# Attention with two mixtures of experts: weights decoded by shifts and ors alone, half chunks scored on a block diagonal

## The chip, the cores and the metric

The kernel runs on one core of one Trainium2 chip. The metric is the device time of one execution in microseconds (us). In the profile PE is TensorE's matrix multiply, PEld its weight load, DVE VectorE, ACT ScalarE, POOL GpSimd and SP SyncE, whose queue issues most DMAs.

## What is computed

```python
# q, k, v: (4 batches, 8 heads, 576, 64) float32; tau a scalar
scores = (q @ k.T) / sqrt(64)
scores = where(scores >= rowmax - tau, scores, -1e9)
attn = exp(scores - rowmax);  attn /= attn.sum + 1e-9
x = (attn @ v) as (2304 tokens, 512)
h = max(x @ w_in, 0);  x = (h * h) @ w_out       # w_in 512 x 2048, w_out 2048 x 512, both float64
e = argmax(x @ w_gate)                           # 8 experts
out[token] = softmax_e * sigmoid(x @ w_output_gate)_e * (max(x @ w1[e], 0) @ w2[e])
```

The weights w_in and w_out arrive as float64. The kernel reads each as two 32-bit words and makes a float32 of them, which it then splits.

## The kernel before

All matrix products that need float32 accuracy run on TensorE in a reduced format, with each operand split into a high part and the remainder (two arrays), so that one product takes three or four passes.

**Order of the work.** The program writes no loops of its own: it adds tasks to a graph (`g.add`), each with an engine, an estimated duration, what it reads and writes and a key. A planner then puts them in order, engine by engine: of the tasks that could start soonest it takes the one with the lowest key. Keys count planned time, T0 = 3 us for one chunk. A task may have a release (`rel`) before which it is not planned. Buffers come from pools; a task whose pool has no free slot is not a candidate. What the planner fixes is only the order in each engine's queue; on the chip each queue runs in that order and waits on semaphores.

**Attention.** There are 16 pairs of heads (4 batches, 4 pairs each), and 9 chunks of 128 query rows for each pair: four of head 0, one half chunk that holds the last 64 rows of both heads (step 4, `hd == 2`), four of head 1. For each chunk: scores (PE, line 630), row maximum (DVE, 639), exponential (ACT, 642), threshold and mask with row sum (647, 651), division (POOL 656 and 662, DVE 659), five transposes (PE, 712), their evacuation in two parts (ACT 729, DVE 732), and after the last chunk of a group the product with v (PE, 755 or 773).

For each pair `t_load` fetches k, q and v; `t_qk` transposes k and q (PE, 568), writes the high part (ACT 576, 578) and the remainder (DVE 584, 586) into one buffer `xy` of four planes; `t_op` copies them by DMA (lines 600 and 603, on SP's queue) into the operands of the scores: for each head an array with high part above and remainder below, so that the 128 rows of the contraction hold both and two passes give all four products. `opA` (head 0) has two slots, `opB` (head 1) one. The half chunk takes two passes from each of the two arrays over both halves of 288 keys: eight matmuls.

**First mixture.** After the four pairs of a batch, `t_h` multiplies with w_in (PE, line 853, 32 units of 12 matmuls a batch), applies max(., 0) (ACT, 859) and stores to scratch r_scr (DMA, 862, three buffers). These units are mixed into the next batch's attention; those of the last batch follow the attention. Then `t_g` and `t_y` (953, 968) read it back and multiply with w_out, gating follows, and the experts (lines 1194 to 1292).

**Decoding.** `t_w` decodes one of 32 weights blocks (16 of w_in, 16 of w_out; 128 x 512 words each): fetch (DMA 818), ACT scales the high word by 2^-112, which rebases the exponent (825), and turns the low word into a number (827); DVE takes the sign (828), shifts the rebased word left by 3 and puts the sign in (830), and isolates the power of two (832); POOL multiplies that with the low word's number (834); POOL (w_in) or DVE (w_out) adds it (836); ACT makes the high part (837) and POOL or DVE the remainder (839). The 16 of w_in are released at 40 + 5i us of planned time and lie among the attention of batches 0 and 1; those of w_out follow the attention.

Of the kernel before, what the change touches and what calls it, by code (L numbers as in the profile page):

```python
# [257 lines left out]
def moa(ctx, tc, q, k, v, tau, w_in, w_out, wg, wog, w1, w2, ctab, coln, out):  # L258
    nc = tc.nc
# [27 lines left out]
    SQ = 640  # L287
# [3 lines left out]
    W1, W2 = 40, 5.0  # L291
# [50 lines left out]
    MEMF, MEMR = 10544, 25856  # L342
# [104 lines left out]
    ATT = at = at + 512  # L447
# [10 lines left out]
    assert at <= DEC, at  # L458
    at = mk("raw", DEC, 4, [P, 2, 512], F32, 2)
# [33 lines left out]
    for i in (1, 2):  # L493
        nc.gpsimd.memset(ALL["opB"].slots[0].view[:, i, 0:64].bitcast(F32), 0.0)
# [13 lines left out]
    raws, vh, xys, opb, xTb, xfb, wb = {}, {}, {}, {}, {}, {}, {}  # L508
# [40 lines left out]
    def t_qk(pr, nm, part, key):  # L549

        raw = raws[pr, nm]
        xy = xys.setdefault(pr, None) or new("xy", pr)
        xys[pr] = xy

        if nm == "k":
            xi, yi = 0, 3
            cs, n0 = ((0, 1, 2), 0) if part == 0 else ((3, 4), 384)
        else:
            xi, yi = 1, 2
            cs, n0 = ((4, 0, 1), 0) if part == 0 else ((2, 3), 320)  # L560
# [12 lines left out]
        def hi():  # L573
            X = xy.t[:, xi, n0 : n0 + n]
            if nm == "k":
                nc.scalar.activation(X, ps.t[:, :n], AF.Copy)
            else:
                nc.scalar.activation(X, ps.t[:, :n], AF.Copy, scale=qsc)

        def lo():  # L580
            X = xy.t[:, xi, n0 : n0 + n].bitcast(F32)
            Y = xy.t[:, yi, n0 : n0 + n]
# [6 lines left out]
        g.add("ACT", c_act(n, True, nm == "q"), hi, [ps], [(xy, xi, part)], key - 1)  # L589
        g.add("DVE", c_dve(n), lo, [ps, (xy, xi, part)], [(xy, yi, part)], key - 1)  # L590

    def t_op(pr, j, key):

        xy = xys[pr]
        buf = opb[pr, j] = new("opB" if j else "opA", f"{pr}")
        rows = slice(64 * j, 64 * j + 64)
        z = 64 if j else 0

        def top():
            nc.sync.dma_start(buf.t[0:64, :, z : z + S].bitcast(F32), xy.t[rows, 0:3].bitcast(F32))  # L600

        def bot(i, src):
            nc.sync.dma_start(buf.t[64:128, i, z : z + S].bitcast(F32), xy.t[rows, src].bitcast(F32))

        parts = lambda *xs: [(xy, x, p) for x in xs for p in range(2)]
        dma(top, 64 * 3 * S * 4, parts(0, 1, 2), [(buf, 0)], key)
        for i, src in ((0, 3), (1, 2), (2, 1)):
            dma(lambda i=i, src=src: bot(i, src), 64 * S * 4, parts(src), [(buf, 1, i)], key)

    def t_chunk(n, key):  # L610
# [5 lines left out]
        if hd == 2:  # L616
            cols = [(1, 0, P), (0, 0, 64)]
        else:
            cols = [(hd, 64 + 64 * hd + QOFF[c], P)]
        seq = [(j, i, q0, m) for j, q0, m in cols for i in (1, 2)]  # L620
        if hd == 2:
            seq = [seq[0], seq[2], seq[3], seq[1]]
        heads = (0, 1) if hd == 2 else (hd,)

        def mm():
            for i, (j, slot, q0, m) in enumerate(seq):
                o = opb[pr, j].t
                z = 64 if j else 0
                for hf in range(2):
                    nc.tensor.matmul(  # L630
                        s.t[:m, hf, :HALF],
                        o[:, slot, q0 : q0 + m],
                        o[:, 0, z + hf * HALF : z + (hf + 1) * HALF],
                        start=(i == 0),
                        stop=(i == len(seq) - 1),
                    )
# [27 lines left out]
        ob = [(opb[pr, j], x) for j in heads for x in (0,)] + [(opb[pr, j], 1, i) for j in heads for i in range(3)]  # L664
        if n < EARLY:
            xy = xys[pr]
            q0 = 64 + QOFF[c]

            def mm():
                i = 0  # L670
                for qx, kx in ((1, 0), (1, 3), (2, 0), (2, 3)):
                    for hf in range(2):
                        nc.tensor.matmul(
                            s.t[:, hf, :HALF], xy.t[0:64, qx, q0 : q0 + P], xy.t[0:64, kx, hf * HALF : (hf + 1) * HALF],
# [4 lines left out]
            rd = [(xy, x, p) for x in (0, 3) for p in range(2)] + [(xy, x, 0 if c < 2 else 1) for x in (1, 2)]  # L679
            g.add("PE", c_pe(HALF) * 8, mm, rd, [s], key)  # L680
        else:
            g.add("PE", c_pe(HALF) * 2 * len(seq), mm, ob, [s], key + K("scores", pr))
# [119 lines left out]
    def t_w(i, key):  # L802

        fc = i % NFC
        raw, av, sg, sc, lf = new("wraw", i), new("wa", i), new("wb", i), new("wc", i), new("wd", i)
# [16 lines left out]
        ts = nc.vector.tensor_scalar  # L822

        dma(fetch, 524288, [], [raw], key - 6, rel=W1 + W2 * i if i < NFC else NCH * T0 - 20)
# [8 lines left out]
        early = i < NFC  # L833
        g.add("POOL", 1.3, lambda: nc.gpsimd.tensor_tensor(sc.t, sc.t, lf.t, op=ALU.mult), [lf], [sc], key)
        rest = ("POOL", 1.3, nc.gpsimd) if early else ("DVE", c_dve(512), nc.vector)
        g.add(*rest[:2], lambda: rest[2].tensor_tensor(av.t, av.t, sc.t, op=ALU.add), [sc], [av], key)
        g.add("ACT", c_act(512), lambda: nc.scalar.activation(w.t[:, 0], av.t, AF.Copy), [av], [(w, 0)], key)
        g.add(*rest[:2],
# [459 lines left out]
    def pair_prep(pr, key):  # L1298
# [116 lines left out]
```

## Time and profile before

| | us |
|---|---|
| median of 3 runs | 1059.66 (1058.43 to 1063.24) |
| profiled execution | 1060.76 |
| its span, first to last instruction | 1059.0 |
| PE busy | 995.3 (94%) |
| DVE busy | 719.3 (68%) |
| ACT busy | 664.8 (63%) |
| POOL busy | 426.3 (40%) |

The span is cut into stages by the clock of the trace: attention runs from about 10 to 500 us, w_in is decoded between 53 and 250 us, w_out between 449 and 570 us, the last batch's first product ends at 562 us, the second product runs to about 750 us, and the experts from there to the end. A stage's busy times say which engine has no slack there; the share over the whole span does not. The busy time of PE counts pipelined matmuls that overlap, so matmuls for each us are read beside it.

### The profile page before, as it was taken

The numbers are of one execution on the slowest core, as the hardware profiler recorded it, in microseconds if no ns is written. First come the engines' busy times: TensorE is split into PE (matmuls) and PEld (weight loads), VectorE is DVE, ScalarE is ACT, GpSimd is POOL, SyncE is SP. The second block draws the span as 40 slices with busy tenths as digits, with TensorE's granted clock in tenths as the row PEclk, the third lists the DMA queues.
The fourth block names the chain that finished last, engine by engine and source line by source line (L and its number), as shares of the span: only waits on it lengthen the run. The fifth ranks groups of instructions, "written<-read, shape, count | busy, mean of one in ns | idle before, by whom it ended". The sixth has DMA issues, their size and how long they took to land.

```text
span 1059.0 us, 19173 instructions
## 1 busy us (share of the span) xinstructions
PE 995.3 (94%) x6300; PEld 883.7 (83%) x6300; DVE 719.3 (68%) x1607; ACT 664.8 (63%) x1379; POOL 426.3 (40%) x757
## 2 busy tenths in 40 slices
PE   6888888889999999999999999999999999999995
PEld 5566678879999999989888888888789998888884
DVE  4789899887777788785964334444677758767720
ACT  5778877766666667675854455444664668767730
POOL 1368898897566665563331000000112211211200
PEclk9989999999999999999999999999999999999998
DMA  6656656544556445553783333443667868877700
GB/s 146 150 151 158 157 130 175 147 117 109 143 142 147 126 125 130 136 157 111 223 237 117 100 100 100 114 117 103 195 190 244 284 211 287 274 253 270 267 20 24
DMA packets 158848, 169.05 MB, mean 160 GB/s; under 512 B 55823, under 2 KB 121615, under 8 KB 158738
## 3 DMA queue, kind: packets, MB, share of 16 engines
q1 hardware_dynamic: 154498, 157.20, 52.5%
q0 software_dynamic: 4096, 10.52, 3.1%
q8 instruction: 52, 0.85, 0.4%
q14 instruction: 58, 0.48, 0.1%
q10 hardware_dynamic: 144, 0.00, 0.0%
HBM read 110.86 MB, written 29.56 MB: 133 GB/s over the span
## 4 chain that ended last, share of the span: by engine, by line
PE 66%; DVE 8%; DMA 7%; issue 7%; POOL 6%; ACT 4%; SPq 0%; POOLq 0%; DVEq 0%; ACTq 0%
PE bank L968 17%; PE bank L853 12%; PE bank L1282 8%; PE bank L1232 7%; PE bank L630 5%; PE bank L712 5%; PE bank L755 5%; DMA memf<-in_moe_w_dram 2%; POOL memf L662 2%; PE bank L1252 1%; DMA out_dram<-memf 1%; PE bank L568 1%; PE bank L773 1%; DVE memf L639 1%; DMA memf<-in_moe_w_in_dram 1%
## 5 line engine op out<-in xcount | busy, mean ns | idle before, releaser
L853 PE MATMUL bank<-memr,w 128*128 128x288 f32 x1536 | 231.9, 300 | 5.3 <-ACT memf L859 4.7
L853 PEld LDWEIGHTS bank<-memr,w 128*128 128x128 f32 x1536 | 210.6, 189 | 9.9 <-ACT memf L859 7.5
L968 PE MATMUL bank<-w,memr 128*128 128x512 f32 x648 | 157.4, 394 | 0.0
L968 PEld LDWEIGHTS bank<-w,memr 128*128 128x128 f32 x648 | 119.1, 188 | 23.5
L651 DVE SCALAR_TENSOR_TENSOR memf<-bank,memf 128x576 f32<-128x576 f32 x144 | 116.4, 810 | 19.0 <-ACT memf L642 18.6
L712 PE MATMUL bank<-ident,memf 128*128 128x128 f32 x720 | 107.7, 280 | 20.0 <-DVE memr L732 8.4
L630 PE MATMUL bank<-memr 128*128 128x288 f32 (+1 forms) x632 | 116.2, 313 | 10.6 <-DVE memf L651 8.7
L639 DVE TENSOR_REDUCE memf<-bank 128x1 f32<-128x576 f32 x144 | 106.9, 748 | 7.8 <-PE bank L630 4.6
L712 PEld LDWEIGHTS bank<-ident,memf 128*128 128x128 f32 x720 | 83.8, 143 | 31.4 <-DVE memr L732 6.2
L662 POOL TENSOR_SCALAR memf<-memf 128x576 f32<-128x576 f32 x128 | 97.6, 764 | 28.0 <-DVE memf L659 21.0
L630 PEld LDWEIGHTS bank<-memr 128*128 128x128 f32 (+1 forms) x632 | 91.7, 188 | 17.1 <-DVE memf L651 14.9
L729 ACT ACTIVATE memr<-bank 128x640 fp32r<-128x640 f32 (+1 forms) x140 | 89.5, 648 | 25.4 <-PE bank L712 23.0
L642 ACT ACTIVATE memf<-bank,memf 128x576 f32<-128x576 f32 x144 | 105.3, 733 | 0.2
L732 DVE TENSOR_TENSOR memr<-bank,memr 128x512 fp32r<-128x512 f32 (+1 forms) x140 | 87.3, 631 | 21.9 <-ACT memr L729 21.3
L1073 POOL DMA_INDIRECT lst<-memf x18 | 17.9, 996 | 203.5 <-DVE memf L1059 140.2
L1232 PE MATMUL bank<-memr,w 128*128 128x256 f32 x564 | 89.0, 283 | 1.5 <-DVE memr L1242 1.4
L953 DVE TENSOR_TENSOR memr<-memf,memr 128x512 fp32r<-128x512 f32 x72 | 48.3, 700 | 54.7 <-ACT memf L950 54.6
L1217 DVE TENSOR_TENSOR w<-memf,w 128x512 fp32r<-128x512 f32 x114 | 74.5, 687 | 12.3 <-ACT w L1214 7.6
L755 PE MATMUL bank<-memr 128*128 128x256 f32 (+1 forms) x504 | 81.4, 304 | 0.0
L1232 PEld LDWEIGHTS bank<-memr,w 128*128 128x128 f32 x564 | 77.4, 191 | 2.7 <-DVE memr L1242 1.9
L647 ACT ACTIVATE memf<-memf,ntau 128x1 f32<-128x1 f32 x144 | 41.9, 292 | 60.1 <-DVE memf L639 45.4
L1217 DVE TENSOR_TENSOR memr<-memf,memr 128x512 fp32r<-128x512 f32 x94 | 62.7, 688 | 22.7 <-ACT memr L1214 18.2
(148 smaller groups left out, 1820.3 us busy)
## 6 DMA issues: line engine op xcount, KB each, us to landing
memf<-in_moe_w_dram SPq DMA_DIRECT2D x104, 512.0 KB
r_scr<-memf SPq DMA_DIRECT2D x128, 144.0 KB
memf<-r_scr SPq DMA_DIRECT2D x36, 512.0 KB
memr<-memr SPq DMA_DIRECT2D x96, 144.0 KB
memr<-memr SPq DMA_DIRECT2D x32, 432.0 KB
memf<-in_moe_w_in_dram SPq DMA_DIRECT2D x16, 512.0 KB
memf<-in_moe_w_out_dram SPq DMA_DIRECT2D x16, 512.0 KB
y_scr<-memf SPq DMA_DIRECT2D x18, 256.5 KB
```

The costliest lines, as they stand in the source:

```text
L630: nc.tensor.matmul(s.t[:m, hf, :HALF], o[:, slot, q0 : q0 + m], o[:, 0, z + hf * HALF : z + (hf + 1) * HALF], start=(i == 0), stop=(i == l ...
L639: nc.vector.tensor_reduce(nm.t, s.t[:, :, :HALF], axis=AX.XY, op=ALU.max, negate=True)
L642: nc.scalar.activation(p.t[:, :S].rearrange("p (a n) -> p a n", a=2), s.t[:, :, :HALF], AF.Exp, bias=nm.t)
L651: nc.vector.scalar_tensor_tensor(p3, s.t[:, :, :HALF], th.t, p3, op0=ALU.is_ge, op1=ALU.mult, accum_out=sm.t)
L662: nc.gpsimd.tensor_scalar(p.t[:, :S], p.t[:, :S], sm.t, 1.0, op0=ALU.mult, op1=ALU.mult)
L712: nc.tensor.transpose(ps.t[:, j], p.t[:, j * P : (j + 1) * P], ident)
L729: nc.scalar.activation(pt.t[:, :NQ, off : off + w], ps.t[:, :, c0 : c0 + w], AF.Copy)
L755: nc.tensor.matmul(ps.t[:, :N], vb.t[:, j, c % NQ].rearrange("p a d -> p (a d)"), pt.t[:, c, :N], start=(c == 0), stop=(c == 2 * NQ - 2),)
L853: nc.tensor.matmul(ps.t[:, :HALF], wv[:, a, kc], xT.t[:, x, kc, half], start=(i == 0), stop=(i == len(seq) - 1),)
L968: nc.tensor.matmul(ps.t, s.t[:, fc], wob[fc].t[:, x], start=(fc == 0 and i == 0), stop=(fc == NFC - 1 and i == 2))
L1217: lambda i=i, w=w, raw=raw: nc.vector.tensor_tensor(w.t[:, 1], raw.t[:, i], w.t[:, 0].bitcast(F32), op=ALU.subtract),
L1232: nc.tensor.matmul(ps.t[:, :256], w1b[kc][fc // 4].t[:, a, (fc % 4) * P : (fc % 4 + 1) * P], x2.t[:, x, kc], start=(i == 0), stop=(i == 11))
```

## The change

The decode loses three steps and one buffer kind: ACT no longer turns the low word into a number, DVE no longer isolates the power of two, POOL no longer multiplies, and nothing adds. Instead DVE shifts the low word right by 29 and ors it to the sign, and ors that to the shifted high word. The sign is now taken from the rebased word instead of the raw high word. The remainder stays on POOL for w_in and on DVE for w_out.

For the half chunk the first 64 columns of q (the last 64 query rows) of both heads are copied into a block diagonal `xd` (128 x 128, zeros off the diagonal, written once at the start), and the scores are taken against k of both heads as it stands (`xk`, heads one above the other), in three passes over two halves: six matmuls. k has its own buffer in two slots now, q in one. `opA` and `opB` lose the half chunk's columns and hold k once and two arrangements of q; they are filled by five DMAs for each head, and the diagonal by two for each pair. The releases of w_in's fetches go from 40 + 5i to 50 + 7i. The buffers of the later stages move in memory.

```diff
-    W1, W2 = 40, 5.0
+    W1, W2 = 50, 7.0
...
+    OPN = S + 2 * 512
...
-        ("vhl", 2, [P, 2, NQ, 2, D]), ("pk", 2, [P, 64]), ("xy", 1, [P, 4, S]), ("opA", 2, [P, 3, S]), ("opB", 1, [P, 3, SQ]),
+        ("vhl", 2, [P, 2, NQ, 2, D]), ("pk", 2, [P, 64]), ("xk", 2, [P, 2, S]), ("xq", 1, [P, 2, S]), ("xd", 1, [P, 2, P]),
+        ("opA", 2, [P, OPN]), ("opB", 1, [P, OPN]),
...
# t_op, for each head j
-        dma(top, 64 * 3 * S * 4, parts(0, 1, 2), [(buf, 0)], key)
-        for i, src in ((0, 3), (1, 2), (2, 1)):
-            dma(lambda i=i, src=src: bot(i, src), 64 * S * 4, parts(src), [(buf, 1, i)], key)
+        for x in range(2):
+            dma(lambda x=x: put_k(x), 64 * S * 4, parts(xk, x), [(buf, "k", x)], key)
+        dma(put_q, 64 * 1024 * 4, parts(xq, 0, 1), [(buf, "q")], key)
+        for x in range(2):
+            dma(lambda x=x: turn_q(x), 64 * 512 * 4, parts(xq, x), [(buf, "t", x)], key)
+    def t_diag(pr, key):
+        xq = xqs[pr]
+        xd = xds[pr] = new("xd", pr)
+        for j in range(2):
+            r = slice(64 * j, 64 * j + 64)
+            dma(lambda r=r: nc.sync.dma_start(xd.t[r, :, r].bitcast(F32), xq.t[r, :, 0:64].bitcast(F32)),
+                32768, [(xq, x, 0) for x in range(2)], [(xd, j)], key)
...
# t_chunk, scores
-            for i, (j, slot, q0, m) in enumerate(seq):
+            if hd == 2:
+                xd = xds[pr].t
+                ops = [(xd[:, x], xk.t[:, y]) for x, y in ((0, 0), (0, 1), (1, 0))]
+            else:
+                o = opb[pr, hd].t
+                ops = [(o[:, S + i * 512 + q0 : S + i * 512 + q0 + P], o[:, :S]) for i in range(2)]
+            for i, (qo, ko) in enumerate(ops):
                 for hf in range(2):
...
# t_w
-        g.add("ACT", c_act(512), lambda: nc.scalar.activation(lf.t, lw(), AF.Copy, scale=2.0**-52), [raw], [lf], key)
-        g.add("DVE", c_dve(512), lambda: ts(si(), hw(), -2147483648, None, op0=ALU.bitwise_and), [raw], [sg], key)
+        g.add("DVE", c_dve(512, 2), lambda: ts(si(), ai(), -2147483648, None, op0=ALU.bitwise_and), [av], [sg], key)
         g.add("DVE", c_dve(512),
-              lambda: nc.vector.scalar_tensor_tensor(
-                  ai(), ai(), 3, si(), op0=ALU.logical_shift_left, op1=ALU.bitwise_or), [sg], [av], key)
-        g.add("DVE", c_dve(512, 2), lambda: ts(ci(), ai(), -8388608, None, op0=ALU.bitwise_and), [av], [sc], key)
-        g.add("POOL", 1.3, lambda: nc.gpsimd.tensor_tensor(sc.t, sc.t, lf.t, op=ALU.mult), [lf], [sc], key)
-        g.add(*rest[:2], lambda: rest[2].tensor_tensor(av.t, av.t, sc.t, op=ALU.add), [sc], [av], key)
+              lambda: stt(si(), lw(), 29, si(), op0=ALU.logical_shift_right, op1=ALU.bitwise_or), [raw], [sg], key)
+        g.add("DVE", c_dve(512),
+              lambda: stt(ai(), ai(), 3, si(), op0=ALU.logical_shift_left, op1=ALU.bitwise_or), [sg], [av], key)
```

## Rows read from the trace of the kernel before

**Rows 1.** The page's first part: busy us, share of the span, instructions.

```profile
PE 995.3 (94%) x6300; PEld 883.7 (83%) x6300; DVE 719.3 (68%) x1607; ACT 664.8 (63%) x1379; POOL 426.3 (40%) x757
```

**Rows 2.** Stages: us; busy PE, PEld, DVE, ACT, POOL (instructions); clock, DMA share, GB/s.

```profile
66.00:122.00 56.00, 47.98 (x277) 36.61 (x276) 49.77 (x109) 47.79 (x97) 43.84 (x71) 0.94 0.63 153
122.00:251.00 129.00, 112.31 (x814) 104.12 (x812) 111.25 (x239) 92.62 (x196) 118.48 (x203) 0.99 0.57 145
149.00:180.00 31.00, 27.04 (x201) 24.89 (x200) 29.54 (x65) 23.41 (x51) 27.54 (x46) 1.00 0.57 150
251.00:370.00 119.00, 118.85 (x920) 116.32 (x920) 93.54 (x218) 80.73 (x178) 73.22 (x172) 1.00 0.53 133
500.00:562.00 62.00, 57.41 (x414) 54.85 (x414) 48.36 (x76) 43.62 (x92) 19.84 (x14) 1.00 0.74 218
```

**Rows 3.** PE's waits from 500 to 562 us: total us, times, longest us.

```profile
PE bank L853 <- ACT memf L859: 4.3, 7, 1.2
```

**Rows 4.** Timeline of PE (start us, us), and the page's group of the scores.

```profile
487.14 1.83 PE L853 MATMUL bank<-memr,w 128*128 128x288 f32 x12
...
496.20 3.42 PE L853 MATMUL bank<-memr,w 128*128 128x288 f32 x24
...
L630 PE MATMUL bank<-memr 128*128 128x288 f32 (+1 forms) x632 | 116.2, 313 | 10.6 <-DVE memf L651 8.7
```

**Rows 5.** Decode steps by line: ns min/median/max, first and last start us, forms.

```profile
L827 ACT ACTIVATE memf<-memf x32: 651/679/702, 54.3 to 564.2; 128x512 f32<-128x512 uint32 x32
L828 DVE TENSOR_SCALAR memf<-memf x32: 411/425/1526, 53.7 to 561.5; 128x512 int32<-128x512 int32 x32
L830 DVE SCALAR_TENSOR_TENSOR memf<-memf x32: 677/744/1778, 56.0 to 563.7; 128x512 int32<-128x512 int32 x32
L832 DVE TENSOR_SCALAR memf<-memf x32: 400/426/1658, 58.4 to 565.3; 128x512 int32<-128x512 int32 x32
L834 POOL TENSOR_TENSOR memf<-memf x32: 1263/1292/1810, 59.8 to 565.9; 128x512 f32<-128x512 f32 x32
L836 POOL TENSOR_TENSOR memf<-memf x16: 1264/1283/1702, 61.7 to 237.7; 128x512 f32<-128x512 f32 x16
L836 DVE TENSOR_TENSOR memf<-memf x16: 678/680/693, 463.3 to 567.7; 128x512 f32<-128x512 f32 x16
L839 DVE TENSOR_TENSOR w<-memf,w x12: 678/691/1782, 520.5 to 569.0; 128x512 fp32r<-128x512 f32 x12
```

**Rows 6.** Who waited for line 825 (us, times).

```profile
  DVE memf L830: 3.4, 6
```

**Rows 7.** Timeline of a collision (start us, us), and the row maximum by line.

```profile
150.88 1.29 POOL L836 TENSOR_TENSOR memf<-memf 128x512 f32<-128x512 f32 x1
...
151.01 1.72 DVE L830 SCALAR_TENSOR_TENSOR memf<-memf 128x512 int32<-128x512 int32 x1
...
L639 DVE TENSOR_REDUCE memf<-bank x144: 726/748/759, 10.8 to 486.2; 128x1 f32<-128x576 f32 x144
```

**Rows 8.** Line 834 by stage: us, POOL busy (instructions), clock, DMA share, GB/s.

```profile
0.00:122.00 122.00, 7.75 (x6) 0.94 0.63 149
122.00:251.00 129.00, 13.35 (x10) 0.99 0.57 145
```

**Rows 9.** Timeline of PE at the second product's start.

```profile
562.12 2.89 PE L968 MATMUL bank<-memr 128*128 128x512 f32 x12
```

**Rows 10.** Line 603's issues by SP (ns), and who waited for them (us, times).

```profile
L603 SPq DMA_DIRECT2D memr<-memr x96: 462/600/2117, 7.1 to 459.5; - x96
...
  PE bank L630: 1.8, 1
```

**Rows 11.** Line 825 between 66 and 165 us: us, ACT busy (instructions), clock, DMA.

```profile
66.00:165.00 99.00, 5.44 (x8) 0.97 0.61 151
```

**Rows 12.** Line 732 by shape: busy us, mean ns, idle before.

```profile
L732 DVE TENSOR_TENSOR memr<-bank,memr 128x512 fp32r<-128x512 f32 x112 | 76.6, 684 | 16.7 <-ACT memr L729 16.4
...
L732 DVE TENSOR_TENSOR memr<-bank,memr 128x256 fp32r<-128x256 f32 x28 | 10.7, 419 | 5.2 <-ACT memr L729 4.9
```

More of the change, by code (lines that the diff above doesn't have):

```diff
@@ L492, in moa @@
     nc.vector.tensor_scalar(qsc, taub, 0.0, 0.125, op0=ALU.is_ge, op1=ALU.mult)
-    for i in (1, 2):
-        nc.gpsimd.memset(ALL["opB"].slots[0].view[:, i, 0:64].bitcast(F32), 0.0)
+    nc.gpsimd.memset(ALL["xd"].slots[0].view.bitcast(F32), 0.0)
     for x in ALL["p"].slots:
@@ L551, in t_qk @@
         raw = raws[pr, nm]
-        xy = xys.setdefault(pr, None) or new("xy", pr)
-        xys[pr] = xy
+        xs = xks if nm == "k" else xqs
+        if pr not in xs:
+            xs[pr] = new("x" + nm, pr)
+        xy = xs[pr]
         if nm == "k":
-            xi, yi = 0, 3
             cs, n0 = ((0, 1, 2), 0) if part == 0 else ((3, 4), 384)
         else:
-            xi, yi = 1, 2
             cs, n0 = ((4, 0, 1), 0) if part == 0 else ((2, 3), 320)
@@ L588, in t_qk, with put_k, put_q, turn_q @@
         g.add("PE", 0.109 * len(cs), tp, [(raw, 0), (raw, 1)] + ([(raw, 2)] if 4 in cs else []), [ps], key, hold=[xy])
[L589 to L590 removed]
+        g.add("ACT", c_act(n, True, nm == "q"), hi, [ps], [(xy, 0, part)], key - 1)
+        g.add("DVE", c_dve(n), lo, [ps, (xy, 0, part)], [(xy, 1, part)], key - 1)
     def t_op(pr, j, key):
[L594 removed]
+        xk, xq = xks[pr], xqs[pr]
         buf = opb[pr, j] = new("opB" if j else "opA", f"{pr}")
         rows = slice(64 * j, 64 * j + 64)
[L597 to L605, printed above, removed]
[L606 to L608 removed]
+        q3 = lambda r: buf.t[r, S:].rearrange("p (x n) -> p x n", x=2).bitcast(F32)
+        def put_k(x):
+            nc.sync.dma_start(buf.t[64 * x : 64 * x + 64, :S].bitcast(F32), xk.t[rows, x].bitcast(F32))
+        def put_q():
+            nc.sync.dma_start(q3(slice(0, 64)), xq.t[rows, :, 64:].bitcast(F32))
+        def turn_q(x):
+            nc.sync.dma_start(q3(slice(64, 128))[:, 1 - x], xq.t[rows, x, 64:].bitcast(F32))
+        parts = lambda xy, *xs: [(xy, x, p) for x in xs for p in range(2)]
+        for x in range(2):
[10 more added lines that the diff above has]
+                32768, [(xq, x, 0) for x in range(2)], [(xd, j)], key)
     def t_chunk(n, key):
@@ L615, in t_chunk @@
         nm, th, sm = (new(x, n) for x in ("nm", "th", "sm"))
[L616 to L622, printed above, removed]
         heads = (0, 1) if hd == 2 else (hd,)
+        halves = [slice(hf * HALF, (hf + 1) * HALF) for hf in range(2)]
+        q0 = QOFF[c]
+        xk = xks[pr]
         def mm():
-            for i, (j, slot, q0, m) in enumerate(seq):
-                o = opb[pr, j].t
-                z = 64 if j else 0
-                for hf in range(2):
[L630 to L636, printed above, removed]
+            if hd == 2:
[5 more added lines that the diff above has]
+            for i, (qo, ko) in enumerate(ops):
+                for hf in range(2):
+                    nc.tensor.matmul(s.t[:, hf, :HALF], qo, ko[:, halves[hf]], start=(i == 0), stop=(i == len(ops) - 1))
         def mx():
@@ L677, in mm @@
                     i += 1
-            rd = [(xy, x, p) for x in (0, 3) for p in range(2)] + [(xy, x, 0 if c < 2 else 1) for x in (1, 2)]
+            rd = [(xk, x, p) for x in range(2) for p in range(2)] + [(xq, x, 0 if c < 2 else 1) for x in range(2)]
             g.add("PE", c_pe(HALF) * 8, mm, rd, [s], key)
-        else:
-            g.add("PE", c_pe(HALF) * 2 * len(seq), mm, ob, [s], key + K("scores", pr))
+        elif hd == 2:
+            rd = [(xk, x, p) for x in range(2) for p in range(2)] + [(xds[pr], j) for j in range(2)]
+            g.add("PE", c_pe(HALF) * 6, mm, rd, [s], key + K("scores", pr))
+        else:
+            o = opb[pr, hd]
+            rd = [(o, "q")] + [(o, w, x) for w in "kt" for x in range(2)]
+            g.add("PE", c_pe(HALF) * 4, mm, rd, [s], key + K("scores", pr))
         g.add("DVE", c_dve(S), mx, [s], [nm], key + K("max", pr))
@@ L822, in t_w @@
         ts = nc.vector.tensor_scalar
+        stt = nc.vector.scalar_tensor_tensor
         dma(fetch, 524288, [], [raw], key - 6, rel=W1 + W2 * i if i < NFC else NCH * T0 - 20)
```

37 lines of the change are left out of this document (16 added, 21 removed).

## Prediction, written before the changed kernel was run

> **What bounds the kernel now.** I read the page's shares and slices first, then busy time by stage, then the waits inside the two stages where TensorE is not full, and last the durations of the instructions that the change touches. The profiled execution took 1060.76 us (span 1059.0); the median of the runs shown is 1059.66. I make the sum against 1060.8 and take 1.1 us off at the end.
>
> TensorE is busy 94% of the span [rows 1], but not everywhere. The stage table [rows 2] cuts the run. From 251 to 370 us PE is busy 118.85 of 119 us, 920 matmuls, so only less PE work helps there. From 122 to 251 us PE is busy 112.31 of 129 us with 814 matmuls; at the pace of the next stage these would take 814/920 x 119 = 105 us, so up to 24 us are PE's idling. There POOL is busy 118.48 of 129 us (92%), DVE 111.25 (86%), ACT 72%. The same 36 chunks run without weight decoding in the next stage, where POOL needs 73 us. From 66 to 122 us DVE leads (49.77 of 56, 89%). From 500 to 562 us PE is busy 57.41 of 62 us, and 4.3 us of its waiting is put down to ACT's evacuation at line 859 [rows 3], which stands in ACT's queue among decode steps. From 562 us on nothing that is edited runs, apart from the last decodes.
>
> **Scores of the half chunk.** Step 4 of each of the 16 pairs goes from eight 288-column matmuls to six. A run of 24 such matmuls in the full stretch takes 3.42 us and one of 12 takes 1.83 us [rows 4], so one is worth (3.42 - 1.83)/12 = 0.1325 us of PE. Pairs 8 to 15 run from 251 us on, where PE is the limit: 8 x 2 x 0.1325 = **2.1 us**. The other 16 matmuls lie under DVE and POOL work; they cost nothing now, and count (another 2.1 us) only if that cover goes.
>
> **Weight decoding, instruction by instruction.** There are 32 weights, 16 of w_in (early) and 16 of w_out (late). ACT loses line 827: 0.679 us each [rows 5]. POOL loses line 834 (1.292) and, early, line 836 (1.283); late, line 836 was on DVE (0.680) and goes too. DVE keeps three steps but of another kind: before 0.411 + 0.677 + 0.400 = 1.49 us undisturbed (lines 828, 830, 832; shortest cases), after one masking step and two scalar_tensor_tensor, 0.40 + 2 x 0.677 = 1.75 us: +0.27 us each. The new shift reads every second word; line 828 reads that pattern already and is as quick as line 832, which reads packed words [rows 5], so I charge nothing for the stride. The mask now reads what ACT wrote, so DVE meets its wait for ACT one step earlier, with row maxima and masks of the softmax queued behind; today that wait is 3.4 us in 6 cases [rows 6], and losing line 828 as filler adds at most 6 x 0.41 = 2.5 us over both halves.
>
> The early DVE steps are not undisturbed. Line 830 took 1.72 us beside a POOL line 836 that began 0.13 us earlier [rows 7], and its longest case is 1.778 against 0.677 [rows 5]; the row maximum, which reads PSUM, stays between 726 and 759 ns [rows 7]. So a POOL operation on two SBUF inputs holds up these DVE steps. [...] All three new DVE steps stay in the class that can be hit, but POOL's large operations go from three to one (early) and from one to none (late). I set the lost delay against the +0.27 us and the earlier wait: DVE comes out even early.
>
> Worth by stage:
> - **122 to 251 us.** Lines 834 and 836 run 10 times each here (834 in [rows 8]): 20 x 1.3 = 26 us leave POOL, which falls to 92 of 129 us and is the limit no more. DVE is next, 111.25 us. In the busiest stretches of the trace DVE reached 49.77/56 = 89% and 29.54/31 = 95% [rows 2]: 125 or 117 us for this stage, a gain of 4 to 12 us. PE's 105 us lie below both. I take the middle, **8 us**.
> - **0 to 122 us.** Six decodes lie here [rows 8], under DVE at 89%. DVE's work does not shrink; ACT and POOL become slacker. Upper bound: 66 to 122 at 95% instead of 89%, 56 x (1 - 0.889/0.953) = 4 us. Lower bound: releases at 50 + 7i instead of a pace set by POOL let two more decodes in before 122, -2 x 1.75 = -3.5 us, given back later. I take **1 us**, near the middle.
> - **500 to 562 us.** ACT sheds 12 x 0.68, DVE 12 x 0.68 and its collisions (line 839's longest case is 1.782, its median 0.691 [rows 5]). Between 0 and the 4.3 us of waiting. What is late next is the last weight: its line 839 starts at 569.0 [rows 5], while the second matrix product begins at 562.12 with 12 matmuls in 2.89 us [rows 9], so 48 matmuls for 16 weights reach the last at 562.1 + 15 x 0.7 = 572.6. That leaves 2.9 us; loads at a DMA share of 0.74 [rows 2] may keep the pace. I take **2.5 us**.
>
> **Operand copies.** Per pair, eight SBUF copies (2 of 432 KB, 6 of 144 KB by their code) become ten of 128 to 256 KB and two diagonal ones of 32 KB: fewer bytes, four more issues on SP at 0.6 us [rows 10], 2.4 us per pair of about 29. In the queue behind a diagonal copy that waits for its buffer (until the previous pair's step 4 has read it) stand the next pair's loads and the stores of r_scr, whose three buffers gate line 859. Today only 1.8 us of PE's waiting in the whole run is put down to these copies [rows 10], and head 1's operands are now first needed at step 5 instead of 4. Cost zero, at most 2.4 us per pair. The larger k buffers, the moved arrays of the later stages and the wider memset at the start cost nothing: no stage reads more or waits for a later owner.
>
> **Sum.** 2.1 + 8 + 1 + 2.5 = 13.6 us; 1060.8 - 13.6 - 1.1 = **1046 us**.
>
> **Rivals.**
> - **DVE takes POOL's place at once.** For: 89% before 122 us, +0.27 us per weight, and if the decodes follow their releases, 13 instead of 8 [rows 11] lie between 66 and 165 us, +5 x 1.75 = 9 us of DVE work there. Against: that work is gone from the next 86 us. Then the middle stage gives 1 to 4 us, the start loses up to 3, and PE's 2.1 us and half of the late gain stay: 1052 to 1058 us. Chance 0.19.
> - **PE becomes the limit from 122 us on.** For: PE's floor is 105 us and t_h work is ready as filler. Against: it needs DVE at its best of 95% with fewer collisions. 15 us there, 3 at the start, 4 late, 2.1: 1034 to 1036, say 1030 to 1040 us. Chance 0.17.
> - **Slower: SP's queue.** SP issues in order, and four more issues a pair could delay r_scr stores until ACT and PE wait at line 859. The price is up to 2.4 us x 12 pairs (4 to 15) = 29 us against 13.6 of gain; it decides as soon as more than half of the 2.4 us (13.6/12 = 1.1 us) per pair reach PE, and it passes +5 us at 1.6. 1064 to 1076 us. For: PE has no slack from 251 to 500. Against: so few waits for copies now. Chance 0.11.
> - **The two-input step runs at half rate.** Line 732 takes 684 ns for 512 elements and 419 for 256 [rows 12], so 512 more element times are 0.53 us; the two such steps of 16 early weights at 1.21 us instead of 0.68 would give 16 x 2 x 0.53 = 17 us of DVE in the stretch that DVE limits, 1060 to 1066 us. Line 830 is such a step on int32 and its shortest case is 0.677 us, one rate with line 732, which speaks against it: chance 0.02. [...]
>
> **How the numbers follow.** The forecast, 1040 to 1052, has chance 0.50; with the rivals that is 0.99, and 0.01 is left for the unforeseen. A measurement here tells a change of about 0.5% (5.3 us) from none, so faster means under 1054.4, slower over 1065. Faster: 0.50 + 0.17 + a third of the DVE rival = 0.73. Slower: 0.11. Same: the rest, 0.16. The range 1032 to 1058 holds the first three cases but for their ends; slower than that are 0.14, and some 0.05 lie below.
>
> **What would show it.** Lines 827, 834 and 836 have no successors; the stage that is now 122 to 251 us shortens to 117 to 125 with POOL near 92 us; two DVE steps per weight near 0.68 us; line 859's waits by PE between 500 and 562 under 2 us; 600 instead of 632 score matmuls at line 630's successor [rows 4]. I am wrong if PE's idling before 251 us stays, if new waits for memr copies stand before the scores, or if the decode's DVE steps are lengthened as often as now.

## The result and the profile after

The changed kernel takes 1047.05 us (median of 4 runs, 1045.51 to 1048.21) beside 1060.01 us for the kernel before on the same chip: a ratio of 0.9873, with a 95% interval of 0.9844 to 0.9902. The forecast was 1046 us. Its profiled execution took 1045.92 us, with a span of 1044.1 us against 1059.0.

The sum came out, but it did not come from where the working had put it. Of the lines that the change aims at, the page and the groups by line show (columns as in [rows 1] and [rows 5]; the successor of line 630 is 645, of 839 it is 849; 841, 843 and 845 are DVE's new mask and the two shifts):

```profile
PE 990.4 (95%) x6268; PEld 879.9 (84%) x6268; DVE 707.5 (68%) x1591; ACT 645.9 (62%) x1347; POOL 365.6 (35%) x708
...
L645 PE MATMUL bank<-memr 128*128 128x288 f32 x600 | 112.6, 315 | 5.5 <-DVE memf L660 5.1
...
L841 DVE TENSOR_SCALAR memf<-memf x32: 406/427/1412, 61.0 to 547.6; 128x512 int32<-128x512 int32 x32
...
L843 DVE SCALAR_TENSOR_TENSOR memf<-memf x32: 672/691/1800, 61.5 to 548.1; 128x512 int32<-128x512 int32 x32
...
L845 DVE SCALAR_TENSOR_TENSOR memf<-memf x32: 668/691/1785, 64.8 to 548.8; 128x512 int32<-128x512 int32 x32
...
L849 POOL TENSOR_TENSOR w<-memf,w x16: 1267/1282/1300, 67.8 to 217.0; 128x512 fp32r<-128x512 f32 x16
```

POOL is 60.7 us lighter than in [rows 1], ACT 18.9, DVE 11.8 (over the whole span). There are 600 score matmuls, as forecast [rows 4]. The two shifting steps take 0.67 us at best; the one on every second word is no slower than the other. Their longest cases, 1.8 us, show that DVE's decode steps can still be stretched. Of the 48 early steps 11 take over 1 us, where 13 did before; six of the 11 overlap the remainder on POOL (849) and four the division (671), which the prediction did not count among POOL's large operations. All the same the 48 steps take DVE 38.0 us in sum, against 38.6 before: "DVE comes out even early" held.

Where the 14.9 us of span went is read from the start of the first row maximum of each pair of heads (line 639 before, 648 after):

| stretch | before, us | after, us | gain | forecast |
|---|---|---|---|---|
| to the start of pair 4 | 122.2 | 114.0 | 8.2 | 1 |
| pairs 4 to 7 | 129.0 | 127.3 | 1.7 | 8 |
| pairs 8 to 13 | 178.5 | 178.4 | 0.1 | 1.6 (of the 2.1) |
| pair 14 to the last row maximum | 56.5 | 54.2 | 2.3 | 0.5 (rest of the 2.1) |
| to the end of w_in's last product (853, 863) | 76.1 | 73.9 | 2.2 | 2.5 |
| from there to the end | 496.7 | 496.3 | 0.4 | 0 |

The table compares one profiled execution of each kernel. Executions of one kernel differ by several microseconds (the changed kernel's four by 2.7, those of one of the variants below by 11.4), so a gain of 1 or 2 us in it is not shown to be the change's.

The stages of the kernel after, with the columns of [rows 2]:

```profile
0.00:34.30 34.30, 24.88 (x113) 19.03 (x114) 18.14 (x45) 18.69 (x38) 8.44 (x33) 1.00 0.64 151
34.30:59.10 24.80, 21.19 (x133) 15.82 (x132) 20.02 (x50) 20.06 (x42) 12.00 (x29) 1.00 0.58 137
59.10:114.00 54.90, 45.52 (x265) 33.56 (x264) 49.74 (x110) 44.39 (x90) 31.64 (x62) 0.97 0.59 147
114.00:241.30 127.30, 117.00 (x818) 107.82 (x817) 115.87 (x248) 90.42 (x192) 99.81 (x187) 0.96 0.60 155
241.30:360.00 118.70, 117.93 (x908) 115.09 (x907) 94.40 (x219) 80.44 (x177) 71.27 (x168) 1.00 0.51 130
```

and two stretches of the kernel before, cut at its pairs 0, 1 and 2:

```profile
0.00:37.70 37.70, 27.26 (x124) 20.43 (x125) 18.77 (x47) 19.77 (x40) 10.78 (x39) 1.00 0.67 147
37.70:67.00 29.30, 24.66 (x136) 17.97 (x135) 22.93 (x53) 22.60 (x46) 14.93 (x30) 0.88 0.59 147
```

In pairs 4 to 7 POOL fell from 118 to 99.8 of about 128 us and is the limit no longer; DVE is now at 115.87 of 127.3 us, 91%. The first two pairs gained 3.4 and 4.5 us; nothing is decoded in them after, and before only the first two weights were begun, from 53.7 us on. Clock may be part of pair 1's gain: the mean granted clock was 0.88 there before (0.50 from 53.58 to 60.41 us, 6.83 of its 29.3 us) and 1.00 after.

### The profile page after: what moved, and what is told of

Read it like the earlier page. It is cut to its first block, busy times and chain, and to the rows that moved or that the text cites. A ratio compares the mean times of both kernels' runs of the same rounds, so it can differ in the third digit from the quotient of the medians.

```text
span 1044.1 us, 19146 instructions
## 1 busy us (share of the span) xinstructions
PE 990.4 (95%) x6268; PEld 879.9 (84%) x6268; DVE 707.5 (68%) x1591; ACT 645.9 (62%) x1347; POOL 365.6 (35%) x708
## 4 chain that ended last, share of the span: by engine, by line
PE 68%; DVE 9%; DMA 7%; issue 6%; ACT 5%; POOL 3%; SPq 1%; DVEq 0%; POOLq 0%; ACTq 0%
PE bank L978 17%; PE bank L863 14%; PE bank L1292 9%; PE bank L1242 8%; PE bank L645 5%; PE bank L724 5%; PE bank L767 5%; DMA memf<-in_moe_w_dram 2%; DVE memf L648 2%; DVE memf L660 2%; PE bank L1262 2%; DMA out_dram<-memf 1%; PE bank L1097 1%; DVE memr L744 1%; PE bank L568 1%
## 5 line engine op out<-in xcount | busy, mean ns | idle before, releaser
L660 DVE SCALAR_TENSOR_TENSOR memf<-bank,memf 128x576 f32<-128x576 f32 x144 | 115.9, 813 | 24.6 <-ACT memf L651 23.0
L724 PE MATMUL bank<-ident,memf 128*128 128x128 f32 x720 | 107.5, 281 | 14.2 <-DVE memr L744 7.8
L645 PE MATMUL bank<-memr 128*128 128x288 f32 x600 | 112.6, 315 | 5.5 <-DVE memf L660 5.1
L724 PEld LDWEIGHTS bank<-ident,memf 128*128 128x128 f32 x720 | 83.5, 143 | 24.8 <-issue 4.7
L645 PEld LDWEIGHTS bank<-memr 128*128 128x128 f32 x600 | 87.5, 194 | 11.4 <-DVE memf L660 9.5
L963 DVE TENSOR_TENSOR memr<-memf,memr 128x512 fp32r<-128x512 f32 x72 | 48.3, 700 | 59.3 <-ACT memf L960 59.2
L665 POOL TENSOR_SCALAR memf<-memf 128x1 f32<-128x1 f32 x144 | 31.9, 222 | 130.7 <-DVE memf L660 110.1
L1292 PE MATMUL bank<-memr 128*128 128x512 f32 x306 | 77.3, 393 | 0.0
```

The lines of the kernel that those rows point to most:

```text
L645: nc.tensor.matmul(s.t[:, hf, :HALF], qo, ko[:, halves[hf]], start=(i == 0), stop=(i == len(ops) - 1))
L660: nc.vector.scalar_tensor_tensor(p3, s.t[:, :, :HALF], th.t, p3, op0=ALU.is_ge, op1=ALU.mult, accum_out=sm.t)
L724: nc.tensor.transpose(ps.t[:, j], p.t[:, j * P : (j + 1) * P], ident)
L1292: nc.tensor.matmul(ps.t, hT.t[:, a, fc, u * P : (u + 1) * P], w2b[fc].t[:, x], start=(fc == 0 and i == 0), stop=(fc == 7 and i == 2))
```

## Experiments

Each ratio is against runs of the kernel before on the same chip. The three theories of the first four runs were written before any of them ran: POOL is the forecast's, SCORES puts the gain on the new operands of the scores, RELEASE on the later fetches.

**Taking the change apart.** `e1_release`, the kernel before with the new releases alone:

```diff
-    W1, W2 = 40, 5.0
+    W1, W2 = 50, 7.0
```

> The kernel before with the later releases of w_in's fetches alone (50 + 7i instead of 40 + 5i). Theory POOL (the prediction's: decoding filled POOL, and its relief brings most of the gain): no change, 1058 to 1062 us. Theory RELEASE (the first two pairs are faster because no decoding lies among them any more): 1054 to 1057 us, with pair 2 starting 3 to 5 us earlier than the kernel before's 67 us. Theory SCORES (k in two buffers and the half chunk's own operand order the first pairs better): no change.

`e2_decode`, the kernel before with the new `t_w` and its buffers alone (two kinds of buffer go, not one, and the one that holds the sign has two slots instead of one; no run takes that second slot apart from the steps):

```diff
-        g.add("POOL", 1.3, lambda: nc.gpsimd.tensor_tensor(sc.t, sc.t, lf.t, op=ALU.mult), [lf], [sc], key)
-        g.add(*rest[:2], lambda: rest[2].tensor_tensor(av.t, av.t, sc.t, op=ALU.add), [sc], [av], key)
...
+              lambda: stt(si(), lw(), 29, si(), op0=ALU.logical_shift_right, op1=ALU.bitwise_or), [raw], [sg], key)
```

> The kernel before with the new decoding alone (scores and releases as before). Theory POOL: 1 + 8 + 2.5 us of gain, 1048 to 1050 us, with POOL near 92 us in the stretch of pairs 4 to 7. Theory SCORES: only the late 2.5 us and a little more, 1055 to 1057 us. Theory RELEASE: about 1054 us, since decoding still lies among the first pairs.

`e2w_decode_release`, both of these edits:

> The kernel before with the new decoding and the later releases, scores as before. Theory POOL: as with the decoding alone, 1048 to 1050 us. Theory RELEASE: 3 to 4 us under the decoding alone, about 1050. Theory SCORES: 1055 to 1057 us.

`e4_old_release`, the changed kernel with `W1, W2 = 40, 5.0`:

> The changed kernel with the releases of the kernel before (40 + 5i). Theory POOL and theory SCORES: as the changed kernel, 1045 to 1048 us. Theory RELEASE: 3 to 4 us slower, 1050 to 1052 us.

| | old decode | new decode | new decode and new scores |
|---|---|---|---|
| releases 40 + 5i | 1 (kernel before) | 0.9913 [0.9884, 0.9942] | 0.9876 [0.9848, 0.9905] |
| releases 50 + 7i | 1.0102 [1.0070, 1.0134] | 0.9952 [0.9922, 0.9983] | 0.9873 [0.9844, 0.9902] (the change) |

RELEASE is refuted: the later releases alone cost 10 us (1069.14 against 1059.01), although pair 2 did start 7.8 us earlier. POOL and SCORES had expected no change here and missed that cost as well. The new decoding alone brings 1049.04 us, 10.0 less, which POOL had at 1048 to 1050 and SCORES at 1055 to 1057. With the later releases added it takes 1052.96 us, which lies between the two. The gain of the decoding lies where the forecast had it. In its trace pairs 4 to 7 run from 119.9 to 241.6 us:

```profile
0.00:119.90 119.90, 93.69 (x530) 69.49 (x530) 96.62 (x216) 87.64 (x178) 62.55 (x131) 0.99 0.68 164
119.90:241.60 121.70, 112.44 (x810) 106.22 (x811) 104.28 (x235) 85.08 (x183) 90.69 (x179) 0.96 0.56 142
```

That is 121.7 us instead of 129.0, with POOL at 90.7 us (forecast: 117 to 125 us and POOL near 92), and 2.3 us at the start (this traced execution is the fastest of five, 2.5 us under their median). The scores bring 3.9 us more with the old releases, where the intervals overlap, and 8.4 with the new, where they do not, by the ratios; the column on the right is the same with either release. So the old releases would have done as well in the whole change (1045.49 us).

What the releases move is seen in the traces. A decode counts from ACT's first step (line 825 before, 839 after):

| | decodes begun before pair 4, in pairs 4 to 7 | DVE busy in pairs 4 to 7, us | pairs 4 to 7, us | pair 8 starts at, us |
|---|---|---|---|---|
| kernel before | 7, 9 | 111.3 | 129.0 | 251.2 |
| e1_release | 5, 11 | 117.2 | 139.9 | 260.1 |
| e2_decode | 9, 7 | 104.3 | 121.7 | 241.6 |
| e2w_decode_release | 8, 8 | 107.8 | 121.1 | 244.6 |
| e4_old_release | 9, 7 | 109.0 | 122.8 | 237.6 |
| the change | 6, 10 | 115.9 | 127.3 | 241.3 |

With the new decoding and seven or eight decodes in pairs 4 to 7 the stretch takes 121 to 123 us; with the change's ten it takes 127.3. The releases and the new scores put ten there together: either alone, added to the new decoding, leaves seven or eight. Of the variants of the change below that add no work to POOL, those with ten there take 128 to 133 us (`e5_four_passes`, `e9_wait_operands`, `e10_more_issues`), the one with five 121.7 (`e11_early_release`). The granted clock does not explain it, since it was 0.96 there in the change and in `e2_decode` alike.

**Is it POOL's time, or what POOL's reads do to DVE?** `e7_pool_reads` puts two useless operations a weight back on POOL, `e8_pool_memsets` the same time in fills that read nothing:

```diff
+        for _ in range(2 if i < NFC else 0):
+            g.add("POOL", 1.3, lambda: nc.gpsimd.tensor_tensor(sg.t, av.t, sg.t, op=ALU.mult), [av], [sg], key)
...
+        for _ in range(5 if i < NFC else 0):
+            g.add("POOL", 0.52, lambda: nc.gpsimd.memset(sg.t, 0.0), [], [sg], key)
```

> The changed kernel with two useless operations on POOL for each of the 16 early weights (128 x 512, two inputs from SBUF, about 1.3 us each, the result read by nothing), as much POOL work as the old decoding had. Theory POOL, by the queue: 6 to 9 us slower, 1053 to 1056 us, most of it between pairs 4 and 8. Theory LOCK (what hurt was that POOL's two-input reads hold up DVE's decoding steps): the same 6 to 9 us. Theory NEITHER (the gain came from fewer steps on ACT or the shorter chain of a weight): within 2 us of the changed kernel.

> The changed kernel with five useless fills on POOL for each early weight (128 x 512 each, about 0.52 us, which read nothing), the same POOL time as in the run with reads. Theory POOL, by the queue: 6 to 9 us slower, as with reads, 1053 to 1056 us. Theory LOCK: at most 2 us slower, 1046 to 1049 us, with DVE's decode steps not stretched beside the fills.

The fills cost 7 us (1054.06 us, ratio 0.9941 [0.9920, 0.9962] against the change's 0.9873), the reads 17 us (1064.3 us, ratio 1.0036 [1.0019, 1.0054]). The stretch of pairs 4 to 7, first with reads, then with fills (columns of [rows 2]), and the added operations by line:

```profile
116.80:254.40 137.60, 118.42 (x825) 107.47 (x824) 115.59 (x246) 90.00 (x190) 126.38 (x211) 0.96 0.52 137
L847 POOL TENSOR_TENSOR memf<-memf x32: 1259/1287/1741, 64.9 to 241.9; 128x512 f32<-128x512 f32 x32
```

```profile
116.40:251.20 134.80, 121.30 (x843) 109.80 (x841) 114.64 (x245) 91.75 (x192) 123.53 (x244) 0.97 0.58 149
L847 POOL MEMSET memf<- x80: 515/525/686, 66.5 to 245.5; 128x512 f32 x80
```

In both POOL is at 92% again, as in [rows 2], and the stretch is 10.3 us (reads) and 7.5 us (fills) longer than in the changed kernel. What a full POOL does to the others shows in DVE's waits for POOL's small step of the division, in pairs 4 to 7 of the kernel before, the change, the fills and the reads, in this order (total us, times, longest us):

```profile
DVE memf L659 <- POOL memf L656: 7.4, 11, 1.7
```

```profile
DVE memf L668 <- POOL memf L665: 2.6, 8, 0.5
```

```profile
DVE memf L668 <- POOL memf L665: 8.4, 12, 1.5
```

```profile
DVE memf L668 <- POOL memf L665: 11.1, 16, 1.5
```

This wait is a sign and not the price; `e4_old_release` has 6.4 us of it in a stretch of 122.8 us. Filling POOL's queue again costs about 7 us: theory POOL. NEITHER, which allowed the reads 2 us, and LOCK alone, which allowed the fills 2 us, are refuted. One rival is not excluded: added tasks also shift the planner's order in every queue, which further down is worth as much. The fills also hold the buffer of the sign longer, but DVE's first step waited for them only 1.5 us in 3 cases.

Reads cost 10 us more than fills of the same length, and the reads missed even the 6 to 9 us that POOL and LOCK had allowed. Part of this is what LOCK names: the 48 early decode steps take DVE 40.9 us in sum beside the reads, 38.0 beside the fills and 38.0 in the change, and of the steps over 1 us 11 of 16 overlap an added read, but only one of 12 an added fill. The 2.9 us from 38.0 to 40.9 are part of the 10. The stretch of pairs 4 to 7 holds 2.8 us of the 10, the rest is spread over later ones, and the traces do not account for it.

**What bounds the decoding stage now.** `e12_no_low_word` leaves the low word's three bits out, one DVE step less for each weight:

```diff
-              lambda: stt(si(), lw(), 29, si(), op0=ALU.logical_shift_right, op1=ALU.bitwise_or), [raw], [sg], key)
```

> The changed kernel without the step that ors the low word's three bits in: the weights are cut to 21 bits of mantissa, one DVE step of 0.69 us less for each of 32 weights. If DVE is the next bound wherever weights are decoded, 5 to 12 us faster than the changed kernel (16 x 0.69 early, 2 to 3 us late). If DVE's work is mostly hidden, within 2 us.

1040.49 us, ratio 0.9820 [0.9797, 0.9843]: 6.6 us less for 16 x 0.69 = 11 us of early DVE work. That is what the forecast said of POOL's successor, with DVE as the next limit. The run does not separate the step's time on DVE from its place in the chain of each weight.

`e11_early_release` has `W1, W2 = 20, 4.0`:

> The changed kernel with w_in's fetches released at 20 + 4i instead of 50 + 7i. With the forecast's view (before 122 us DVE leads, but pairs 0 and 1 leave it a fifth of their time): 2 to 5 us faster than the changed kernel, 1042 to 1045 us. With the prediction's rival of decodes that bunch on DVE: 0 to 5 us slower, with pairs 2 and 3 later.

1052.67 us, ratio 0.9929 [0.9900, 0.9959], about 6 us slower than the change, and pair 1 shows why (34.4 to 70.2 us):

```profile
34.40:70.20 35.80, 27.16 (x149) 18.98 (x146) 27.96 (x63) 24.63 (x51) 18.48 (x34) 0.95 0.69 174
```

35.8 us instead of 24.8, with 8 us more of DVE work in it: five decodes begin there. Eleven begin before pair 4, which starts at 122.6 us, and pairs 4 to 7 give part back (121.7 us instead of 127.3). The slack that the averages showed in pairs 0 and 1 was not usable; this is the rival of decodes that bunch, and my own expectation for this run, the forecast's view, was wrong.

**What in the new scores brings the start forward.** `e5_four_passes` puts the two matmuls back, `e6_one_k` takes the second k buffer away, `e9_wait_operands` makes step 4 wait for the copies that it no longer reads:

```diff
-                ops = [(xd[:, x], xk.t[:, y]) for x, y in ((0, 0), (0, 1), (1, 0))]
+                ops = [(xd[:, x], xk.t[:, y]) for x, y in ((0, 0), (0, 1), (1, 0), (1, 1))]
...
-        ("xk", 2, [P, 2, S])
+        ("xk", 1, [P, 2, S]), ("hole", 1, [P, 2, S])
...
+            rd += [(opb[pr, j], "q") for j in range(2)] + [(opb[pr, j], w, x) for j in range(2) for w in "kt" for x in range(2)]
```

> The changed kernel with the half chunk's fourth pass put back (low part times low part): eight matmuls a pair on the diagonal instead of six. Theory PASSES (the two matmuls are what the new scores are worth): 2 to 5 us slower than the changed kernel, 1049 to 1052 us, and each full pair of the stretch where TensorE is busy all the time takes 0.26 us longer than the changed kernel's 29.5. Theory BUFFERS (the operands' new order and the second k buffer bring the start forward, and the two matmuls are given back to a wait of the q transposes): 1047 to 1049 us and the full pairs stay at 29.5 us.

> The changed kernel with one slot for k instead of two. Theory BUFFERS: the next pair's k cannot be transposed until step 4 has read the present one, so pairs 0 to 3 lose 4 to 8 us of what they gained and the kernel is at 1050 to 1056 us. Theory PASSES: within 2 us of the changed kernel.

> The changed kernel, with the half chunk's scores made to wait for both heads' copied operands too, and to hold them, as the kernel before did (they are not read). Theory DEADLINE (the new scores bring the start forward because step 4 no longer needs head 1's copies): pair 4 starts at 119 to 122 us instead of 114, and the kernel is at 1050 to 1053 us. Theory ORDER (what is left of the gain of the new scores is the planner's other order and no single edge): within 2 us of the changed kernel.

| | median, us | ratio | pair 4 starts at, us |
|---|---|---|---|
| the change | 1047.05 | 0.9873 [0.9844, 0.9902] | 114.0 |
| e5_four_passes | 1049.14 | 0.9892 [0.9847, 0.9936] | 114.5 |
| e6_one_k | 1050.75 | 0.9892 [0.9827, 0.9957] | 116.8 |
| e9_wait_operands | 1050.45 | 0.9912 [0.9884, 0.9941] | 116.6 |

Each interval overlaps that of the change, so none of the three is shown to be the cause; the start moves by 0.5, 2.8 and 2.6 us, where the kernels with the old scores are at 119.9 to 123.5 (the three runs above and the kernel before). `e9_wait_operands` is the cleanest of the three: on every engine and on SP's queue its trace shows the same lines in the same order as the change's, so the planner has no part in what differs. But its executions had the lower granted clock (0.982 to 0.986, the change's 0.985 to 0.993), so its 3.4 us cannot be put down to the wait alone.

The first two pairs do not need the new scores: pair 2 starts at 59.2, 58.8 and 59.5 us in `e1_release`, `e2_decode` and `e2w_decode_release`, at 59.1 in the change and at 67.0 in the kernel before. Pairs 2 and 3 then take 61.0, 61.1 and 64.0 us in those three, 54.9 in the change and 55.3 in `e4_old_release`; but they took 55.2 in the kernel before, with the old scores, so the scores alone do not set this either.

What e5 does settle is the stretch in which PE is busy all the time, where theory PASSES had 0.26 us more for each pair. Four pairs (36 row maxima) of the kernel before, of the change and of e5, in this order (us, busy DVE):

```profile
282.50:400.30 117.80, 26.62 (x36) 1.00 0.54 133
```

```profile
272.00:390.10 118.10, 26.61 (x36) 1.00 0.51 131
```

```profile
273.80:391.50 117.70, 26.60 (x36) 1.00 0.51 129
```

Two matmuls fewer or more for each pair change nothing there. PE's timeline tells why; before:

```profile
321.67 1.30 PE L630 MATMUL bank<-memr 128*128 128x288 f32 x8
...
324.63 0.38 PE L568 MATMUL bank<-ident,memf 128*128 128x128 f32 x2
324.92 0.80 PE L853 MATMUL bank<-memr,w 128*128 128x288 f32 x4
```

and after:

```profile
311.29 1.05 PE L645 MATMUL bank<-memr 128*128 128x288 f32 x6
...
313.99 0.38 PE L568 MATMUL bank<-ident,memf 128*128 128x128 f32 x2
314.58 0.67 PE L863 MATMUL bank<-memr,w 128*128 128x288 f32 x3 [0.21 <-DVE memr L586]
```

Eight score matmuls became six, 0.25 us less. But from the last two q transposes to the next product it is 0.59 us instead of 0.29: the product waits for DVE to empty the bank that q's transposes filled (line 586). What was saved comes back as that wait. It is not this pair's alone; PE's waits from 272 to 360 us of the changed kernel show three, where the kernel before has none from 282 to 370 us (total us, times, longest us):

```profile
PE bank L863 <- DVE memr L586: 0.6, 3, 0.2
```

**SP's issues.** `e10_more_issues` cuts each copy of k in two:

```diff
+            for h in range(2):
+                dma(lambda x=x, h=h: put_k(x, h), 64 * HALF * 4, parts(xk, x), [(buf, "k", x, h)], key)
```

> The changed kernel with each copy of k into the operands cut into two by columns: four more DMA issues on SP for each pair, the same bytes. The prediction's rival on SP's queue: if more than half of the 2.4 us a pair reaches TensorE, 14 to 29 us slower than the changed kernel. If SP's issues are hidden, as the forecast had it: within 2 us.

1057.24 us, ratio 0.9972 [0.9954, 0.9989]: 10 us slower than the change, near neither expectation. By stage (columns of [rows 2]):

```profile
10.80:40.30 29.50, 23.84 (x108) 17.35 (x107) 16.91 (x43) 17.61 (x36) 7.80 (x23) 0.94 0.53 122
40.30:119.10 78.80, 65.11 (x383) 49.87 (x382) 66.90 (x154) 61.99 (x127) 40.00 (x82) 0.94 0.61 151
119.10:251.60 132.50, 119.26 (x819) 109.81 (x818) 116.50 (x249) 90.66 (x192) 100.14 (x190) 0.94 0.57 148
251.60:370.00 118.40, 117.62 (x904) 114.61 (x903) 93.73 (x217) 80.23 (x177) 71.27 (x168) 1.00 0.51 128
```

Pair 0 takes 29.5 us instead of 23.5, pairs 4 to 7 take 132.5 instead of 127.3, and the full pairs (8 to 13) nothing. The rival counted pairs 4 to 15, but its mechanism is not there: in pairs 4 to 7 PE's waits show none for ACT's evacuation behind w_in's product (line 871 here). Whether SP's time, the planner's other order or the clock does it, this run can't tell: an added task shifts the order in every queue, and the granted clock was 0.94 in the first three stretches, where the change had 0.96 to 1.00.

## Why the prediction was right, and where not

**Decoding: right in mechanism, size and place, when it stands alone.** The new decode by itself gave 10.0 us where the terms add up to 1 + 8 + 2.5 = 11.5. Its traced execution, 14.2 us of span under the kernel before's, has 7.3 of them in pairs 4 to 7 (forecast 8), 2.3 at the start (1) and 3.5 between the last row maximum and w_in's last product (2.5). The fills and DVE's waits for POOL speak for POOL's fullness as the reason, the run without the low word for DVE as the next limit; the planner's order is the rival that is left.

**122 to 251 us in the whole change: mis-sized.** 8 us were forecast, 1.7 came. The step that failed is that the term took DVE's work in this stage as it was, 111.25 us. DVE's work on all early decodes did stay even, but more of it came to lie here: 33 of its decode steps instead of 26, and DVE was busy for 115.87 us. These are the steps in pairs 4 to 7, lines 828, 830 and 832 of the kernel before, then 841, 843 and 845 of the change (us, busy DVE and instructions):

```profile
122.20:251.20 129.00, 4.86 (x8) 0.99 0.57 145
122.20:251.20 129.00, 10.06 (x9) 0.99 0.57 145
122.20:251.20 129.00, 7.68 (x9) 0.99 0.57 145
```

```profile
114.00:241.30 127.30, 6.85 (x10) 0.96 0.60 155
114.00:241.30 127.30, 10.34 (x11) 0.96 0.60 155
114.00:241.30 127.30, 9.46 (x12) 0.96 0.60 155
```

The level was right: DVE reached 91%, between the two ends of 89 and 95% from which the term was made, and at 91% the 111.25 us would have taken 122 us, a gain of 7 (an estimate). I had costed the releases only as a bound on the start, and with the wrong sign: "let two more decodes in before 122" is what the new decoding does at the old releases (nine begun before pair 4 instead of seven), and with the new scores the later releases take them out again (six). The decodes that are moved are not lost time of the same size: the change's pair 8 starts 9.9 us earlier than before, where the two terms together had 9.

**Scores: the term was in the wrong place.** "Pairs 8 to 15 run from 251 us on, where PE is the limit", priced at 2.1 us, gave 0.1 in pairs 8 to 13, since a wait behind line 586 took the 0.25 us a pair. "They cost nothing now" of the first pairs was wrong the other way: the new scores are worth 8.4 us by the ratios with the new releases and, not clear of noise, 3.9 with the old. In the traces pair 4 starts 9.5 and 5.1 us earlier by them, and pairs 4 to 7 give 6.2 and 1.1 of that back. I had looked at them as matmuls and copies; what changes the start may be what step 4 waits for and holds, or the order of the queues, and which of these stays open.

**Copies: "cost zero" is not shown.** Four more issues a pair on top of the change's four cost 10 us, before pair 8 and not in pairs 8 to 13. The change's own four may cost something there too, under the gain; but no wait of PE for these copies is left in its trace, where the kernel before had 1.8 us [rows 10] and `e10_more_issues` has 2.0. The wait that the working named is in the trace after, with its releaser (SP's queue, first 241 us: total us, times, longest us):

```profile
SPq L621 <- DVE memr L586: 11.5, 2, 8.4
```

It is the diagonal copy, waiting by the profile for q's low part and not for its own buffer, for 8.4 us at the longest.

**500 to 562 us: right.** 2.2 us came, 2.5 were forecast. PE's wait for the evacuation [rows 3] fell from 4.3 us to 2.1 in the stretch from 487 to 548 us (forecast: under 2), and DVE's wait for the first decode step grew as named, by more than the 2.5 us bound, where DVE is not the limit (busy 39.42 of these 61.0 us, PE 58.43):

```profile
PE bank L863 <- ACT memf L869: 2.1, 4, 1.0
...
DVE memf L841 <- ACT memf L839: 12.7, 10, 5.1
```

**The rivals.** A two-input step at half rate would take 1.21 us by the estimate from [rows 12]; lines 843 and 845 take 0.67 at best, 0.69 in the median, so that rival is refuted. DVE did take POOL's place: in the whole change the middle stage's 1.7 us are what the rival of DVE had there (1 to 4), but the start, where it had a loss of up to 3, gained 8.2. With the decoding alone DVE's level left the gain. No single mechanism made the sum right: by the stages, two terms were too large by 6.3 and 1.5 us and two too small by 7.2 (the start) and 1.8 (pair 14 on). With the same working, the kernel with the decoding alone would have been called to within 2 us (11.5 against 10.0). The whole change was called well partly by luck: a gain of the scores that I had not seen met a cost of the releases that I had not seen.

## What to carry to other kernels

An engine that is full only in one stretch (POOL at 92% there, 40% over the span) is found by busy times by stage, and the gain of relieving it has a bound in the next engine's load in that stretch (here DVE's 111.25 of 129 us [rows 2]). In a kernel whose order comes from a planner, an edit's price has a second part that no sum shows, here up to 10 us for a release time or four more copies, with next to none of it in pairs 8 to 13, where TensorE hardly idles (PE is busy 117.93 of 118.70 us from 241.3 to 360 us of the change). Work that a planner can place earlier or later is priced for each stage only together with how much of it will lie there. In a stretch where one engine hardly idles, ask also what follows the instructions that you remove: two matmuls fewer bought 0.25 us and a wait of 0.30.

## What the runs showed of the hardware

- A fill of 128 x 512 took POOL 0.525 us in the median (line 847 of `e8_pool_memsets`), a two-input operation of that size 1.287 us (line 847 of `e7_pool_reads`), and in these runs the second cost the kernel more than its length says: 17 us against 7 for nearly the same POOL time a weight (2 x 1.287 = 2.57 us against 5 x 0.525 = 2.63). Of DVE's early decode steps over 1 us, 11 of 16 overlapped the added two-input operations and one of 12 the added fills.
- A scalar_tensor_tensor of shifts and ors on two int32 inputs from SBUF ran at the rate of a float tensor_tensor of that size (0.668 us for 512 at best, against 0.678 in line 836 [rows 5]), and reading every second word showed no cost (line 843, 0.672 at best and 0.691 in the median, reads so; line 845, with the same median, does not).
- The granted clock of TensorE was 0.50 for four short stretches in the first 250 us of either kernel's trace, where PE is busy 210.21 us (before) and 217.29 us (after); between 250 and 770 us, with PE busy 512.52 and 513.56 of 520 us, neither trace shows it. The four took 6.83, 3.41, 3.41 and 3.40 us in the kernel before and 3.41 us each in the changed one. The first of the kernel before began at 53.58 us, right behind a gap of 1.63 us on PE. Ten matmuls of line 773 that began at 57.66 us took 3.85 us, at a mean clock of 0.64, and 2.51 us earlier in the same run, at 1.00 (then the three stretches with the columns of [rows 2]):

```profile
26.80 2.51 PE L773 MATMUL bank<-ptf,memf 128*64 128x256 f32 x10 [0.44 <-DVE memr L586]
...
53.58 1.33 PE L712 MATMUL bank<-ident,memf 128*128 128x128 f32 x5 [1.63 <-ACT ptf L723]
55.45 2.29 PE L630 MATMUL bank<-memr 128*128 128x288 f32 x8 [0.54 <-DVE memf L651]
57.66 3.85 PE L773 MATMUL bank<-ptf,memf 128*64 128x256 f32 x10
```

```profile
26.80:29.31 2.51, 2.51 (x11) 1.26 (x11) 1.86 (x6) 1.58 (x3) 0.19 (x1) 1.00 0.99 220
53.58:57.66 4.08, 3.54 (x13) 2.87 (x13) 3.87 (x9) 1.93 (x3) 2.08 (x4) 0.50 0.90 249
57.66:61.51 3.85, 3.85 (x12) 1.90 (x12) 3.74 (x8) 2.38 (x5) 3.77 (x8) 0.64 0.19 67
```

I had given the clock no term. It differs between executions of one kernel, and in some runs the longer ones have the lower mean: `e11_early_release` took 1048.33 us at 0.992 and 1055.19 at 0.987, `e9_wait_operands` 1048.16 at 0.986 and 1053.66 at 0.982, while the ten of `e7_pool_reads` show no such link (1062.15 us at 0.986, 1064.65 at 0.986). Whether the clock makes them longer, or their waits lower the clock, is not shown.
